# Two interleaved layers of multi-query attention and SwiGLU: chunks turned by VectorE at the layer change, a chunk's operands made earlier, and implied waits declared away

## The chip, the core and the metric

The kernel runs on one core of a Trainium2 chip. The core's engines work in parallel, each through its own queue in order: TensorE (PE: matrix products and transposes; PEld is its weight load), VectorE (DVE), ScalarE (ACT), GpSimd (POOL) and SyncE (SP, which here issues nearly all DMA transfers). Semaphores order the engines against each other; an instruction that waits holds everything behind it in its queue. The metric is the time of one launch on the device in microseconds (us); the median of several runs counts.

## The reference

The input has 2048 rows of 448 numbers. Two kinds of layer alternate, each on a layernorm of the running sum and added to it:

```python
H, Dh, F = 16, 28, 1792
def _A_ref(x, wq, wk, wv, wo):
    q = (x @ wq).reshape(B, S, H, Dh).transpose(0, 2, 1, 3)
    k = x @ wk
    v = x @ wv
    scores = jnp.einsum("bhqd,bkd->bhqk", q, k) * (Dh ** -0.5)
    o = jnp.einsum("bhqk,bkd->bhqd", softmax(scores), v)
    return o.transpose(0, 2, 1, 3).reshape(B, S, H * Dh) @ wo
def _B_ref(x, w_gate, w_up, w_down):
    return (silu(x @ w_gate) * (x @ w_up)) @ w_down

x = x + _A_ref(_layernorm(x), wq, wk, wv, wo)
x = x + _B_ref(_layernorm(x), w_gate, w_up, w_down)
x = x + _A_ref(_layernorm(x), wq, wk, wv, wo)
x = x + _B_ref(_layernorm(x), w_gate, w_up, w_down)
```

The 16 query heads share one key head and one value head. All is float32; the kernel gets that precision by writing operands as a high part and a low part (names ending in `h` and `l`) and adding three products.

## The kernel before

**Tiling.** Rows are on the partitions of `xres` (16 tiles of 128 rows). The rows fall into four chunks of 512. For a product a chunk must be turned: features on partitions, 512 rows along the free axis. This turned form, in halves, is an `xtile`: `xh` and `xl`, and for the feed-forward `xd`, a tile that holds a second copy of the last 64 features on the upper partitions. There are two ways to make one. `flip` has PE transpose 16 blocks of 128x128 (L248) into PSUM; ACT copies the high half out (L254, L258) and DVE subtracts for the low half (L255, L264). `turn_tile` has DVE transpose a tile of rows in blocks of 32x32 (L268), and four DMAs for each tile (L271) write the blocks to DRAM in their turned order; `rows3` reads the chunk back in three DMAs (L130 and two of L132), and `halved` splits it (L278 to L288), on whichever engines it is given.

**The order.** Each engine's order is the order in which the program calls its instructions; it is written out by hand. The stages follow each other: projection, scores, feed-forward, and the same again for the second layer. There is a second, fuller path for inputs whose softmax sums leave a range; it does not run here.

**Scores.** `scores` runs 128 cycles a layer. A cycle (`cycle`) computes two tiles of scores (128 keys by 4 heads of 512 queries each) on PE (L590) into two PSUM groups of three banks, `threes`, and two single banks. ACT takes the exponentials: of the first tile's single bank (L607) and three banks (L608), of the second tile's three banks (L611) and, since DVE has copied it out (L610), its single (L612). `pv(m - 1)` then multiplies the exponentials of the cycle before with the values (P-V, L639) into the single bank that L607 has just read, and DVE adds that to an accumulator (L646, L648). The exponentials go to buffers `pt` and `pt1`, four of each. Every eighth cycle a group of heads ends; `post` normalises it: sums go out to DRAM and come back (L659, L669, L670), POOL multiplies (L677). Some other work is laid between the cycles, by cycle number: the chunks of the feed-forward are normalised and turned by `turn_tile` for chunks 0 to 2, and chunk 1 is read back near the end (`ff.fetch(1)`).

**Feed-forward.** `unit(gi, c, n)` takes one block of 256 of the 1792 hidden features of chunk c: gate and up products in two halves (L318; with L298 for the chunk-0 units at the start, which don't use `xd`), Silu on ACT (L902), products on DVE (L903, L907), a high half on ACT (L904). The down products of a unit are held back in `pend` and run between the halves of the next unit; each block of PE's work ends with tiny ACT copies of its banks into `seen` (L325), for which PE waits before it writes those banks in the other order. After a chunk's second unit of a group the residual is added: two tiles on DVE (L806), two by ACT and POOL (L809, L810). A list `soon` holds functions with a count of units after which they run, at the end of a unit's calls; `mid` holds functions that run in the middle of a given unit. `rest` starts the stage: a shifted copy for chunk 0 by DMA (L127), chunk 1's operands by ACT and DVE, the read of chunk 2 (`fetch(2)`) and its halves on POOL one unit later, chunk 3 by `flip`.

**Layer change.** In the last group (6) of layer 0's feed-forward, `hand_over(c)` normalises a finished chunk (statistics L217, L218; `rstd` on POOL, L222 and L223; scaling L230) for the next layer's projection. Its scaling runs one unit later, by `soon`. For chunks 0 and 1 the `flip` stands in the middle of the unit (6, c + 2, 0), in two halves, and the projections that use it follow (`a.project()`, two for chunk 0, one for chunk 1). Chunk 2 is turned by `flip` inside the projection. A projection (`project`, `q`) is one block of L298 products, copied out by ACT to `stage` (L523, L524), from where SP writes it to DRAM: queries to `qd` (L525), keys to `kt` (L528). `finish` runs what is left of the projection; before that it calls `fetch` twice, which reads four blocks of queries back (`wrq`, L444) and lets POOL cast them (L446) for the products that bound the scores (`maxima`, L424), which come up in `q` at projection 6.

Of the kernel before, what the change touches and what calls it, by code (L numbers as in the profile page):

```python
# [8 lines left out]
F32 = mybir.dt.float32  # L9
# [46 lines left out]
def forward(  # L56
# [209 lines left out]
    def turn_tile(got, tb, raw, t):  # L266

        nc.vector.transpose(tb[:, t, :], got["x"][:, t, 0:D])  # L268
        to = raw.rearrange("(b d) (t g w) -> t g d b w", d=32, g=4, w=32)
        for g in range(4):  # L270
            nc.sync.dma_start(to[t, g], tb[32 * g : 32 * g + 32, t, :].rearrange("d (b w) -> d b w", w=32))  # L271
# [57 lines left out]
    class Attention:  # L329
# [224 lines left out]
        def scores(self, ff):  # L554
            next(switch)
            with tc.tile_pool(name=f"at{self.layer}", bufs=1, reuse_waits="tile") as wp:
                woh = wp.tile([P, NG, D], F32R, name="woh")
                wol = wp.tile([P, NG, D], F32R, name="wol")
# [24 lines left out]
                def tile_scores(n, three, one):  # L583
# [19 lines left out]
                def cycle(m):  # L603
# [3 lines left out]
                    nc.scalar.activation(pt1, a, AF.Exp, scale=SCALE)  # L607
                    nc.scalar.activation(pt, threes[0], AF.Exp, scale=SCALE)  # L608
                    pt, pt1 = tile_scores(2 * m + 1, threes[1], b)
                    nc.vector.tensor_copy(pt1, b)  # L610
                    nc.scalar.activation(pt, threes[1], AF.Exp, scale=SCALE)  # L611
                    nc.scalar.activation(pt1, pt1, AF.Exp, scale=SCALE)  # L612
# [20 lines left out]
                def pv(m, to):  # L633
# [10 lines left out]
                    if u == 0:  # L644
                        accs[i] = halves("o2").bitcast(F32)
                        nc.vector.tensor_copy(accs[i][:, 0, :], to)  # L646
                    else:
                        nc.vector.tensor_tensor(accs[i][:, 0, :], to, accs[i][:, 0, :], ALU.add)  # L648
# [3 lines left out]
                def post(i):  # L652
# [4 lines left out]
                    rs = wp.tile([P, 16], F32, name="rs", bufs=2)  # L657
# [3 lines left out]
                    def rest():  # L661
                        if fine is not None:
                            under = wp.tile([P, 16], F32, name="under", bufs=2)
# [7 lines left out]
                        if g == 0:  # L671
                            on[c] = (
                                wp.tile([P, NG, 512], F32R, name="onh"),
                                wp.tile([P, NG, 512], F32R, name="onl"),
# [11 lines left out]
                def turns(c, got):  # L686
# [3 lines left out]
                    def one(t):  # L690
                        if t == 0:
                            at_["tb"] = wp.tile([P, 4, D], F32, name="tb")
                        turn_tile(got, at_["tb"], ff.raw[c], t)
# [68 lines left out]
    class FeedForward:  # L762
# [61 lines left out]
        def hand_over(self, c):  # L824

            a = self.nxt
            fs, got = norm_steps(c)
# [3 lines left out]
            a.X[c] = xtile(xpool if c == 0 else self.xbp)  # L831

            def ready():
                for f in fs[5:]:
                    f()
                if c > 1:
                    a.norms[c] = got
# [94 lines left out]

        def rest(self, xb):
            self.stage = xb.enter_context(tc.tile_pool(name=f"stage{self.layer}", bufs=2, reuse_waits="tile"))
            self.xbp = xb.enter_context(tc.tile_pool(name=f"xb{self.layer + 1}", bufs=3, reuse_waits="tile"))
# [8 lines left out]
            self.fetch(2)  # L944
            self.soon.append([0, lambda: self.parts(2, nc.gpsimd.tensor_copy, nc.gpsimd.tensor_tensor)])
# [100 lines left out]
```

## Time and profile before

| | |
|---|---|
| runs | 2002.25, 1998.70, 1998.66 us; median 1998.7 |
| profiled execution | 2002.23 us |
| its span, first to last instruction | 2000.5 us |
| granted clock of TensorE | 0.997 |
| projection of layer 0, to | 64 us |
| scores, layer 0 | 64 to 571 us |
| feed-forward, layer 0 | 571 to 1017 us |
| rest of layer 1's projection | 1017 to 1055 us |
| scores, layer 1 | 1055 to 1561 us |
| feed-forward, layer 1 | 1561 to 2000.5 us |

A line of a timeline gives start, duration, engine, line of the kernel, operation, what it writes and reads, and how many of them follow each other; in brackets how long the engine stood idle before it, and for whom. A line of a list of groups gives the count, busy time and mean duration in ns, and the idle time before the group. `SPq` and `ACTq` are instructions of the queues themselves: DMA issues and waits.

### The profile page before, as it was taken

The page shows a single profiled execution, that of the slowest core. Times are in us where ns is not written, and L with a number is a line of the kernel's source. Part 1 is how long each engine was busy: PE and PEld are TensorE (multiplying, and loading weights), DVE is VectorE, ACT ScalarE, POOL GpSimd, SP SyncE. Part 2 cuts the span into 40 slices and gives each one's busy share as a digit, 9 for nine tenths or more (in the row PEclk, how much of TensorE's full clock was granted, in tenths as well). Part 3 has the DMA queues.
Part 4 walks back from the last instruction along what each step waited for, and adds up shares of the span by engine and source line. Part 5 has one row for each costly group of instructions (what it writes and reads, how often), then busy time and mean ns, then how long its engine had stood idle before and what let it go on. Part 6 is the DMA issues. An engine that isn't in the chain of part 4 may idle for free.

```text
span 2000.5 us, 44597 instructions
## 1 busy us (share of the span) xinstructions
PE 1978.4 (99%) x18517; PEld 1337.5 (67%) x18517; DVE 785.4 (39%) x1370; ACT 1277.5 (64%) x2142; POOL 560.4 (28%) x611
## 2 busy tenths in 40 slices
PE   9999999999999999999999999999999999999998
PEld 7544545445468999999884444454454789988887
DVE  6444443443543222322464334535444332222322
ACT  4899797997953333333349998979979433333332
POOL 5222213122214233333351221122221233233320
PEclk9999999999999999999999999999999999999999
DMA  5101020021211011110031010200212100011102
GB/s 164 52 24 37 12 57 17 22 51 32 44 42 35 25 32 31 32 31 22 12 100 35 25 31 12 62 13 26 52 37 58 45 16 22 26 31 32 32 1 76
DMA packets 126343, 75.30 MB, mean 38 GB/s; under 512 B 69656, under 2 KB 109976, under 8 KB 126136
## 3 DMA queue, kind: packets, MB, share of 16 engines
q1 hardware_dynamic: 124584, 71.20, 12.9%
q8 instruction: 146, 2.39, 0.5%
q10 hardware_dynamic: 1552, 1.20, 0.2%
q14 instruction: 61, 0.50, 0.1%
HBM read 54.01 MB, written 17.83 MB: 36 GB/s over the span
## 4 chain that ended last, share of the span: by engine, by line
PE 94%; DVE 2%; POOL 1%; ACT 1%; DMA 1%; issue 0%; ACTq 0%; POOLq 0%; SPq 0%; DVEq 0%
PE bank L318 39%; PE bank L639 24%; PE three L590 17%; PE bank L590 6%; PE bank L298 4%; PE three L575 2%; PE bank L575 2%; PE bank L248 1%; POOL xl L279 0%; DMA qd<-stage 0%; ACT pt L611 0%; DVE xn L230 0%; DMA xn<-xt 0%; DMA xres<-in_A_x_dram 0%; DVE xres L579 0%
## 5 line engine op out<-in xcount | busy, mean ns | idle before, releaser
L639 PE MATMUL bank<-pt,vsb 128*32 128x512 f32 x4096 | 493.2, 598 | 0.5
L590 PE MATMUL bank<-qstack,keys 32*128 32x512 f32 x1536 | 483.8, 424 | 1.7 <-DVE xres L579 1.7
L590 PE MATMUL three<-qstack,keys 32*128 32x512 f32 x4608 | 448.8, 420 | 1.4 <-ACT stage L524 1.0
L318 PE MATMUL bank<-xh,wgh 64*128 64x512 f32 x1728 | 443.7, 391 | 4.0 <-ACT xh L278 1.4
L590 PEld LDWEIGHTS three<-qstack,keys 32*128 32x128 f32 x4608 | 258.1, 182 | 282.2 <-ACT pt L608 185.2
L611 ACT ACTIVATE pt<-three 128x1536 f32<-128x1536 f32 x256 | 383.1, 1496 | 0.0
L608 ACT ACTIVATE pt<-three 128x1536 f32<-128x1536 f32 x256 | 379.4, 1482 | 0.0
L318 PE MATMUL bank<-xh,wgl 64*128 64x512 f32 x1404 | 366.2, 391 | 0.0
L318 PE MATMUL bank<-wdh,h 64*128 64x448 f32 x1792 | 333.1, 365 | 1.2 <-ACT h L904 0.8
L318 PE MATMUL bank<-xl,wgh 64*128 64x512 f32 x1296 | 331.4, 391 | 2.6 <-POOL xl L279 2.1
L903 DVE TENSOR_TENSOR sg<-bank,sg 128x512 f32<-128x512 f32 x112 | 77.5, 692 | 511.8 <-ACT sg L902 502.6
L318 PEld LDWEIGHTS bank<-xh,wgh 64*128 64x128 f32 x1728 | 261.2, 185 | 22.5 <-POOL xh L288 2.2
L639 PEld LDWEIGHTS bank<-pt,vsb 128*32 128x32 f32 x4096 | 107.1, 109 | 249.1 <-issue 152.6
L810 POOL TENSOR_TENSOR xres<-stage,xres 128x448 f32<-128x448 f32 x108 | 127.9, 1204 | 506.0 <-ACT stage L809 506.0
L648 DVE TENSOR_TENSOR o<-bank,o 128x512 f32<-128x512 f32 x224 | 155.0, 692 | 280.5 <-PE bank L639 276.4
L610 DVE COPY pt<-bank 128x512 f32<-128x512 f32 x256 | 176.9, 691 | 205.5 <-PE bank L590 203.1
L318 PEld LDWEIGHTS bank<-wdh,h 64*128 64x128 f32 x1792 | 244.3, 185 | 14.7 <-issue 2.3
L590 PEld LDWEIGHTS bank<-qstack,keys 32*128 32x128 f32 x1536 | 243.9, 183 | 7.8 <-DVE xres L579 3.6
L677 POOL TENSOR_TENSOR o<-o 128x512 f32<-128x512 f32 x32 | 41.2, 1289 | 739.7 <-DMA o<-rd 431.6
L325 ACT COPY seen<-bank 128x1 f32<-128x1 f32 x664 | 81.4, 163 | 255.0 <-PE bank L318 249.8
L318 PEld LDWEIGHTS bank<-xh,wgl 64*128 64x128 f32 x1404 | 214.7, 185 | 13.1
L318 PE MATMUL bank<-wdl,h 64*128 64x448 f32 x896 | 218.2, 368 | 0.0
(130 smaller groups left out, 2323.5 us busy)
## 6 DMA issues: line engine op xcount, KB each, us to landing
o<-rd SPq DMA_DIRECT2D x32, 256.0 KB
qd<-stage SPq DMA_DIRECT2D x32, 224.0 KB
qraw<-qd SPq DMA_DIRECT2D x128, 56.0 KB
wdr<-in_B_w_down_dram SPq DMA_DIRECT2D x28, 224.0 KB
xt<-tb SPq DMA_DIRECT2D x96, 56.0 KB
wr<-in_B_w_gate_dram SPq DMA_DIRECT2D x28, 192.0 KB
wr<-in_B_w_up_dram SPq DMA_DIRECT2D x28, 192.0 KB
xn<-xt SPq DMA_DIRECT2D x6, 768.0 KB
```

What stands on the lines that cost most here:

```text
L298: nc.tensor.matmul(po, a, b, start=(i == 0), stop=(i == len(seq) - 1))
L318: nc.tensor.matmul(po, a, b, start=start, stop=stop, skip_group_check=True)
L325: nc.scalar.copy(seen[:, i : i + 1], po[:, 0:1])
L575: nc.tensor.matmul(po[:, 0:D], a[:, g, ts_], b[:, g, :], start=(g + z == 0), stop=(g == NG - 1 and z == 2))
L590: nc.tensor.matmul(three[:, j, :] if j < 3 else one, k[js, kp, ks], q[js, part, :], start=(z == 0), stop=(z == 2), tile_position=(32 * j, 0),)
L608: nc.scalar.activation(pt, threes[0], AF.Exp, scale=SCALE)
L610: nc.vector.tensor_copy(pt1, b)
L611: nc.scalar.activation(pt, threes[1], AF.Exp, scale=SCALE)
L639: nc.tensor.matmul(to[32 * j : 32 * j + 32, :], vsb[:, n % NT, :], pts[n][j], start=(y == 0), stop=(y == 1), skip_group_check=True,)
L648: nc.vector.tensor_tensor(accs[i][:, 0, :], to, accs[i][:, 0, :], ALU.add)
L810: nc.gpsimd.tensor_tensor(r, s, r, ALU.add)
L903: nc.vector.tensor_tensor(sg, pg[1], sg, ALU.mult)
```

## The change

It has four parts.

1. At the layer change, chunks 0, 1 and 2 are no longer turned by PE. `hand_over` registers two functions for each: `turn` scales the chunk, turns it by `turn_tile` (DVE, then 16 DMAs) into DRAM and reads it back (3 DMAs); `parts` makes the halves by ACT copies and DVE subtractions. They are called one and two units later, chunk 2's `parts` after projection 5. Chunk 0's two projections are called one unit later than before.
2. At the start of both feed-forwards, `begin` makes chunk 1's operands right after the last exponentials, into a pool of their own (`x1`), before the first unit; chunk 2 is read back one unit earlier, in `scores`, and its halves are issued on POOL at the start of `rest`, ahead of the first unit of chunk 1. The shifted copies of chunks 0 and 1 both go by DMA.
3. In the scores the four buffers `pt` and `pt1` are named tiles, taken in turn, and three kinds of dependency are declared absent, with the reason that another wait implies them: between an exponential and the one that wrote the same buffer two cycles before (and DVE's copy L610 likewise), between the accumulator's addition and the one before it, and between it and an exponential of the next cycle.
4. What outlives the scores' buffers (`woh`, `wol`, `rs`, `onh`, `onl`) sits in a pool `ow` on the other side of the memory, so that the pool `at` can be closed ahead of the feed-forward's first unit.

```diff
     def turn_tile(got, tb, raw, t):
-        nc.vector.transpose(tb[:, t, :], got["x"][:, t, 0:D])
+        nc.vector.transpose(tb, got["x"][:, t, 0:D])
...
-        def scores(self, ff):
+        def scores(self, ff, xb):
...
-                    pt = wp.tile([P, 3, 512], F32, name="pt", bufs=4)
-                    pt1 = wp.tile([P, 512], F32, name="pt1", bufs=4)
+                    pt, pt1 = bufs[n % 4]
...
+                exps, sums = {}, {}
+                bufs = [
+                    (wp.tile([P, 3, 512], F32, name=f"pt{y}"), wp.tile([P, 512], F32, name=f"single{y}"))
+                    for y in range(4)
+                ]
...
-                    nc.scalar.activation(pt1, a, AF.Exp, scale=SCALE)
-                    nc.scalar.activation(pt, threes[0], AF.Exp, scale=SCALE)
+                    es = [nc.scalar.activation(pt1, a, AF.Exp, scale=SCALE)]
+                    es.append(nc.scalar.activation(pt, threes[0], AF.Exp, scale=SCALE))
...
+                    exps[m] = [e.ins for e in es]
+                    for new, old in zip(exps[m], exps.get(m - 2, ())):
+                        tc.declare_no_dep(new, old, reason="P-V, which read the buffer, waited for the old one")
+                    if m > 1:
+                        tc.declare_no_dep(copy.ins, exps[m - 2][3], reason="P-V, which read it, waited for that")
...
+                        if m + 1 in exps:
+                            tc.declare_no_dep(f.ins, sums[m - 1], reason="scores, ahead of this P-V, waited for the sum")
+                    sums[m] = f.ins
+                    if m + 1 in exps:
+                        tc.declare_no_dep(f.ins, exps[m + 1][0], reason="P-V waited for the bank's exponential")
...
+                inner.close()
                 next(switch)
                 ff.X[0] = X0
+                ff.begin(xb)
                 ff.unit(0, 0, 0)
                 due.popitem()[1]()
+                ff.fetch(2)
                 ff.unit(0, 0, 1)
...
         def hand_over(self, c):
             a = self.nxt
-            fs, got = norm_steps(c)
+            fs, got = norm_steps(c, twice=c == NC - 1)
...
-            a.X[c] = xtile(xpool if c == 0 else self.xbp)
+            a.X[c] = xtile((xpool, self.x1p, self.xbp, self.xbp)[c])
...
-            self.soon.append([1, ready])
-            if c < 2:
-                self.mid[len(groups) - 1, c + 2, 0] = [lambda ks=ks: flip(got, a.X[c], ks) for ks in ((0, 1), (2, 3))]
-                self.soon.append([2, lambda: [a.project() for _ in range(2 - c)]])
+            raw = dram.tile([D, 512], F32, name=f"xt1_{c}")
+            def turn():
+                for f in fs[5:]:
+                    f()
...
+                for t in range(4):
+                    turn_tile(got, self.tb[t // 2][:, t % 2, 0:D], raw, t)
+                got["raw"] = pers.tile([P, 4, 512], F32, name="xn")
+                rows3(got["raw"], raw)
+            def parts():
+                halved(a.X[c], got["raw"], range(4), nc.scalar.copy, nc.vector.tensor_tensor)
+            self.soon.append([1, turn])
+            if c == 2:
+                a.plan[5, 1] = [parts]
+                return
+            self.soon.append([2, parts])
+            self.soon.append([3 - c, lambda: [a.project() for _ in range(2 - c)]])
...
+        def begin(self, xb):
+            self.x1p = xb.enter_context(tc.tile_pool(name=f"x1{self.layer}", bufs=1, reuse_waits="tile"))
+            self.X[1] = xtile(self.x1p)
+            halved(self.X[1], self.got.pop(1), range(4), nc.scalar.copy, nc.vector.tensor_tensor)
+
         def rest(self, xb):
...
-            dma(self.xd[0][64:128, :], self.X[0][0][0:64, 3, :])
-            self.X[0] = (*self.X[0][:2], self.xd[0])
-            self.parts(1, nc.scalar.copy, nc.vector.tensor_tensor)
+            for c in range(2):
+                dma(self.xd[c][64:128, :], self.X[c][0][0:64, 3, :])
+                self.X[c] = (*self.X[c][:2], self.xd[c])
...
-            self.fetch(2)
-            self.soon.append([0, lambda: self.parts(2, nc.gpsimd.tensor_copy, nc.gpsimd.tensor_tensor)])
+            self.parts(2, nc.gpsimd.tensor_copy, nc.gpsimd.tensor_tensor)
```

More of the change, by code (lines that the diff above doesn't have):

```diff
@@ L552, in finish @@
             wide.append(LOW)
-        def scores(self, ff):
+        def scores(self, ff, xb):
             next(switch)
-            with tc.tile_pool(name=f"at{self.layer}", bufs=1, reuse_waits="tile") as wp:
-                woh = wp.tile([P, NG, D], F32R, name="woh")
-                wol = wp.tile([P, NG, D], F32R, name="wol")
+            inner = ExitStack()
+            with tc.tile_pool(name=f"ow{self.layer}", bufs=1, side="right", reuse_waits="tile") as ow:
+                wp = inner.enter_context(tc.tile_pool(name=f"at{self.layer}", bufs=1, reuse_waits="tile"))
+                woh = ow.tile([P, NG, D], F32R, name="woh")
+                wol = ow.tile([P, NG, D], F32R, name="wol")
                 on, accs, pts = {}, {}, {}
```

34 lines of the change are left out of this document (19 added, 15 removed).

## The prediction

> **What bounds the kernel now.** I read the page's chain of waits first.
>
> ```profile
> span 2000.5 us, 44597 instructions
> PE 94%; DVE 2%; POOL 1%; ACT 1%; DMA 1%; issue 0%; ACTq 0%; POOLq 0%; SPq 0%; DVEq 0%
> ```
>
> PE is in 94% of the chain that ended last, so work that leaves PE counts in full, and a wait counts where PE stands in it. The scores are a quarter of the program each time, and there I looked closer: at the busy time of the engines in one stretch of them (us; PE, its weight loads, DVE, ACT, POOL), at ACT's timeline, and at the list of the single tile's exponential L607.
>
> ```profile
> 80.00:197.00 117.00, 117.00 (x1273) 50.07 (x1269) 46.83 (x84) 117.00 (x127) 23.09 (x21) 1.00 0.09 24
> ...
> L607 ACT ACTIVATE pt<-bank x33: 604/654/700, 79.7 to 197.7; 128x512 f32<-128x512 f32 x33
> ...
> L607 ACTq EVENT_SEMAPHORE  x254: 17/17/1029, 64.2 to 1556.6; - x127
> ...
> 68.69 0.63 ACT L607 ACTIVATE pt<-bank 128x512 f32<-128x512 f32 x1
> 76.01 0.68 ACT L607 ACTIVATE pt<-bank 128x512 f32<-128x512 f32 x1
> ```
>
> PE and ACT are both busy for all 117 us, so the first row doesn't tell which of them sets the period of a cycle (four exponentials, two tiles). The starts do. Between 79.7 and 197.7 us lie 32 periods, 3.688 us each; the two cycles from 68.69 to 76.01 took 3.66 each. PE's work is the same in both. What the early cycles lack are ACT's waits on itself: the exponentials of cycles 0 and 1 write fresh buffers, and the waiting instructions of L607 number 254 to its 256 exponentials. So ACT, with its waits, sets the period.
>
> **The change part by part.**
>
> *Waits in the scores.* They go from some 126 cycles of each layer: 252 x (3.688 - 3.660) = -6.9 us. Bounds: 0, if PE's P-V after L607's end turns out to be what closes the period, and -8.2 (.0325 a cycle, if the rounding of the starts is all on one side).
>
> *A new wait in layer 0.* The first three-bank exponential now writes a buffer that lies where the projection's staging tile lay, and waits until the last key copy out of it (L528) has landed.
>
> ```profile
> 65.51 1.47 ACT L608 ACTIVATE pt<-three 128x1536 f32<-128x1536 f32 x1
> ...
> 65.72 0.39 SPq L528 DMA_DIRECT2D kt<-stage  x1
> 68.16 0.55 SPq L383 DMA_DIRECT2D wrk<-kt  x1
> ```
>
> That copy is issued at 65.72, and SP's next instruction, which waits for it, goes at 68.16: landed at about 68.0, so the exponential starts 2.5 us late, once. Behind it in ACT's queue stands the whole cycle, and P-V waits for that: +2.5. (0, if PE's work ahead covered it; 3 at most.) In layer 1 the corresponding copies are down in time.
>
> *Start of each feed-forward.* Today PE runs into waits here, on ACT's copy of chunk 1 and on POOL's halves of chunk 2.
>
> ```profile
> 593.71 0.37 PE L575 MATMUL bank<-woh,onl 128*128 128x448 f32 x1
> 594.78 0.50 PE L318 MATMUL bank<-xh,wgh 64*128 64x512 f32 x2 [0.71 <-ACT xh L278]
> 612.90 0.50 PE L318 MATMUL bank<-xl,wgh 64*128 64x512 f32 x2 [1.07 <-POOL xl L279]
> 622.21 0.39 PE L318 MATMUL bank<-xh,wgh 64*128 64x512 f32 x1
> ...
> 1584.42 0.37 PE L575 MATMUL bank<-woh,onl 128*128 128x448 f32 x1
> 1614.12 0.39 PE L318 MATMUL bank<-xh,wgh 64*128 64x512 f32 x1
> ...
> 960.42 0.57 PE L318 MATMUL bank<-xh,wgh 64*128 64x512 f32 x2
> 964.18 0.57 PE L318 MATMUL bank<-xh,wgh 64*128 64x512 f32 x2
> 967.72 0.57 PE L318 MATMUL bank<-xh,wgh 64*128 64x512 f32 x2
> ```
>
> The last three rows, far from any stall, give the normal unit: 7.30 us, 3.76 for its first gate-up half with a down-projection and 3.54 for its second. From the end of the last output projection (593.71 + .37 = 594.08) three units should bring PE to 615.98; it gets there at 622.21, so 6.2 us are lost. Layer 1: 1584.79 + 21.9 = 1606.69 against 1614.12, 7.4 lost. After the change chunk 1's operands are made right behind the last exponentials, while PE multiplies the first unit's weights, so the wait on ACT's L278 goes. Chunk 2's halves are made by POOL from here on:
>
> ```profile
> 600.81 1.01 POOL L223 TENSOR_TENSOR rstd<-rstd,halfn 128x4 f32<-128x4 f32 x1
> 606.52 0.61 POOL L278 CAST xh<-xn 128x512 fp32r<-128x512 f32 x1
> 609.14 1.29 POOL L279 TENSOR_TENSOR xl<-xn,xh 128x512 fp32r<-128x512 f32 x1
> 611.06 1.78 POOL L279 TENSOR_TENSOR xl<-xn,xh 128x512 fp32r<-128x512 f32 x1
> 614.26 1.26 POOL L288 TENSOR_TENSOR xh<-xn,xd 64x512 fp32r<-64x512 f32 x1
> ...
> 611.03 0.69 DVE L907 TENSOR_TENSOR h<-sg,h 128x512 fp32r<-128x512 f32 x1 [0.69 <-ACT h L904]
> ```
>
> They take 606.52 to 615.52, 9.0 us. POOL now issues them right behind L223 and ahead of the residual adds. DVE's statistics lose the four operations ahead of them, so L223 ends some 2.9 us sooner than 601.82: about 598.9, and the halves are ready at 607.9. PE begins with chunk 2 at 594.08 + 2 x 7.30 = 608.7 and, in the order of the rows, wants the last of them some .4 later, near 609.1. What is late next is chunk 1's shifted copy (L127), now behind chunk 0's: issued some .8 after the last output projection's start, landed 2.3 later (as the key copy above) near 596.8, .4 after PE's first use, in each layer. Sum: -(6.2 + 7.4) + .9 = -12.7. Bounds -13.6 and -10.
>
> The row at 611.06 is .49 longer than its like at 609.14, and DVE's product L907 starts beside it at 611.03. [...]
>
> *The hand-over to layer 1.* First what goes: 48 PE transposes and their evictions, in three lumps.
>
> ```profile
> 978.20 0.49 PE L298 MATMUL bank<-xh,wh 128*128 128x512 f32 x1
> 983.43 0.49 PE L318 MATMUL bank<-xh,wgh 64*128 64x512 f32 x2
> 1007.77 0.39 PE L318 MATMUL bank<-xh,wgh 64*128 64x512 f32 x2
> 1025.07 1.10 PE L424 MATMUL bank<-q,kdiag 112*128 112x512 f32 x4
> 1026.00 1.91 PE L248 MATMUL bank<-ident,xn 128*128 128x128 f32 x16
> 1027.67 0.48 PE L298 MATMUL bank<-xh,wh 128*128 128x512 f32 x1
> ```
>
> The unit from 967.72 to 978.20 holds chunk 0's lump: 10.48 - 7.30 = 3.2. Chunk 1's, of the same 16 and two such splits of a unit, I take at the same or a little less, 3.0 (an estimate); chunk 2's is 1027.67 - 1026.00 = 1.7. Together -7.9.
>
> In their place stands, for each chunk, a chain across four queues: DVE's scaling and four transposes, 16 writes and 3 reads on SP, four copies on ACT, four subtractions on DVE. Its pieces are all in the trace, because chunks of the feed-forward go this way already:
>
> ```profile
> 969.48 1.77 DVE L230 TENSOR_SCALAR xn<-xres,mv,rstd 128x448 f32<-128x448 f32 x4
> L268 DVE STREAM_TRANSPOSE tb<-xn 128x448 f32<-128x448 f32 x24 | 15.2, 635 | 0.0
> 288.64 2.25 SPq L271 DMA_DIRECT2D xt<-tb  x4
> 292.31 0.39 SPq L130 DMA_DIRECT2D xn<-xt  x1
> 1588.16 4.75 DMA xn<-xt
> ...
> 984.56 0.42 SPq L528 DMA_DIRECT2D kt<-stage  x1
> 1015.38 2.07 SPq L444 DMA_DIRECT2D wrq<-qd  x4
> 1022.29 2.02 POOL L446 CAST q<-wrq 112x1024 fp32r<-112x1024 f32 x2
> 1015.99 0.47 PE L318 MATMUL bank<-wdh,h 64*128 64x448 f32 x1 [0.18 <-ACT seen L325]
> ```
>
> From scaling to the first turned tile 1.77 + .64 = 2.4; 16 writes at 2.25 / 4 = .56 or, with nothing between them, less, 8.3; from the last write's end to the reads 292.31 - 290.89 = 1.4; the third read goes 1.0 later and lands in 4.75; the last copy .6, the `seen` copies behind it .5. About 19.7 us from the start of scaling.
>
> The place decides what that costs. The copies stand in ACT's queue ahead of the `seen` copies (L325), and PE's second gate-up half waits for those (the last row shows such a wait). Chunk 0: scaling at 969.48, copies through at 989.2. Without its lump PE would reach that half at 967.72 + 7.30 + 3.76 = 978.8. Stall 10.4 (9.8 to 10.9): the two projections (978.20 to 983.43) that could have covered 5.2 of it are moved behind it. Chunk 1: counted from that half's start, its writes can go on SP only behind the copies of those projections: 3.5 to the pair, 6.4 to its last copy (984.56 - 978.20) and .4 for that, 10.3. Then 8 for the writes, 1.5, 1.0, 4.8, and copies to 27.4 or 28.4; PE needs it at 3.5 + 5.2 + 7.3 + 2.6 + 3.8 = 22.5. Stall 5.3 (4.3 to 5.8). Chunk 2: the 16 writes and 3 reads go ahead of the four wrq reads on SP, and behind these stand POOL's L446 and PE's L424, which today runs 17.3 after the last unit's second half starts (1007.77). The writes can start 7.5 after it; with 8 for them, 1.4 until they are down, 1.6 for the reads, .4 for a query copy, 2.1 for the wrq reads, some 3.0 for landing (between the 2.3 of the key copy above and the 4.75) and 1.0 for the last L446, L424 goes at 25.0. Against 17.3, stall 7.7 (6.7 to 8.3). In all 23.4 - 7.9 = +15.5, between 13 and 17.5. POOL's 12 copies L232 go too; nothing waited for them.
>
> **Sum.** +15.5 - 12.7 + 2.5 - 6.9 = -1.6 us. The profiled execution took 2002.23 for its span of 2000.5; its span would be 1998.9. The other two runs took 1998.7, so the profiled one lies 3.5 high; on the median I predict 1998.7 - 1.6 = 1997.1 us.
>
> **The rivals.**
>
> *PE closes the period of the scores (slower).* P-V (L639) is queued ahead of the scores that feed the next L607, and waits for L607: a loop through both engines, and PE is as full as ACT in the stretch above. If that loop, not ACT's row of four, is 3.69 long, it keeps its length and the waits buy nothing: -1.6 + 6.9 = +5.3, 2004.0. It decides if the period stays above 3.68. Against it stand the cycles of 3.66.
>
> *The hand-over costs less (faster).* If PE finds L424 late by nothing, since SP has other slack or the next projections can run ahead of it, chunk 2's 7.7 go: -9.3, 1989.4. For it: PE is in one queue with much work left in that stage; against: L424 stands in that queue where it is, and the wrq reads can't pass the writes on SP.
>
> *The change doesn't do what it says at the feed-forward's start.* If POOL's halves still end where they do, for want of L223 or of the read that is now issued earlier, only the first waits there go, 1.4 a layer: -1.6 + 12.7 - 2.8 = +8.3, 2007.0. The reads are issued some 15 us earlier, so I see little for it.
>
> **How the numbers follow.** The forecast has .48, the cheaper hand-over .26, the scores' loop .18, the late halves .08. No change is told from one within 0.2%, 4 us, of the median: 1994.7 to 2002.7. The forecast's own range is 1992 to 2001, with a quarter of it below 1994.7; faster gets .26 + .12 = .38, slower .08 + .12 of the loop's case + .02 of the forecast's = .22, same the other .40. The range from 1988 to 2006 leaves out half of the late halves and the outermost of the cheap hand-over.
>
> **What would show it.** In the list of exponentials a period of 3.66 right through the layer, not 3.69. At layer 0's first cycle a gap of 2.5 between the first two exponentials. No PE wait on POOL's halves in the first three units of either feed-forward. In the last group of layer 0's feed-forward two stalls of PE on ACT's `seen` copies, 10 and 5 us, and one of about 8 ahead of L424. The forecast is wrong if one of the three large terms is: if the stalls lie elsewhere or are hidden, or the period stays.

## The result, and the profile after

The changed kernel takes 2018.2 us (median of 4 runs, 2016.96 to 2018.95) against 1999.9 for the kernel before (4 runs, 1998.66 to 2002.25): 1.0086 times as long, 95% interval 1.0074 to 1.0098. The prediction was 1997.1 and its range ended at 2006. The profiled execution took 2018.01 us; its span is 15.8 us longer than before, where -1.6 was forecast.

The page after: span, the clock granted to PE in 40 slices of the span (9 is 90% or more), and the chain by engine.

```profile
span 2016.3 us, 43622 instructions
...
PEclk9999999999999999999889999999999999999999
...
PE 95%; DMA 2%; DVE 1%; ACT 1%; issue 0%; SPq 0%; POOL 0%; ACTq 0%; DVEq 0%; POOLq 0%
```

The chain looks as before. What is new is a dent in the granted clock, in the two slices from 958 to 1059 us: the layer change.

Where the time went is read by putting the starts of the same instructions side by side, from the two timelines. Whatever lies between two rows of this table gained or lost the difference of its last column.

| instruction | before, us | after, us | after minus before |
|---|---|---|---|
| first exponential of layer 0 | 65.02 | 65.46 | +0.4 |
| the same of cycle 2 | 72.35 | 76.69 | +4.3 |
| the same of the last cycle, 127 | 565.95 | 568.99 | +3.0 |
| Silu of unit (0,2,0), layer 0 | 621.18 | 618.83 | -2.3 |
| Silu of unit (6,1,1) | 966.86 | 964.52 | -2.3 |
| Silu of unit (6,2,0) | 977.08 | 971.81 | -5.3 |
| Silu of unit (6,2,1) | 989.82 | 991.98 | +2.2 |
| Silu of unit (6,3,0) | 1000.04 | 1005.14 | +5.1 |
| Silu of unit (6,3,1) | 1010.28 | 1023.35 | +13.1 |
| first exponential of layer 1 | 1055.62 | 1079.50 | +23.9 |
| the same of the last cycle | 1556.64 | 1579.17 | +22.5 |
| Silu of unit (0,2,0), layer 1 | 1613.09 | 1629.03 | +15.9 |
| end | 2000.50 | 2016.29 | +15.8 |

So the starts of the two feed-forwards gain 5.4 and 6.6, 12.0 together (12.7 forecast), the scores 1.3 a layer (6.9 forecast for both), the first cycles lose 3.9 (2.5), and the layer change loses 26.2 (15.5). Outside these places the two kernels run in step to .2 us.

The layer change first. These are the waits of PE there (us in total, times, longest), then the row of PE after the first of them, and below it four stretches: their length, busy time of PE, PEld, DVE, ACT and POOL, then the granted clock.

```profile
PE bank L318 <- ACT seen L325: 16.4, 3, 10.5
PE bank L424 <- POOL q L446: 8.3, 1, 8.3
PE bank L298 <- DVE xres L826: 1.4, 1, 1.4
```

```profile
987.30 0.80 PE L318 MATMUL bank<-xh,wgh 64*128 64x512 f32 x2 [10.54 <-ACT seen L325]
987.90 0.63 PE L318 MATMUL bank<-xl,wgh 64*128 64x512 f32 x2
988.32 0.63 PE L318 MATMUL bank<-xh,wgl 64*128 64x512 f32 x2
```

```profile
987.20:990.00 2.80, 2.69 (x12) 2.17 (x14) 1.00 (x2) 0.38 (x5) 0.00 (x0) 0.50 0.00 0
993.00:997.00 4.00, 4.00 (x21) 3.10 (x20) 3.31 (x8) 1.20 (x2) 0.00 (x0) 1.00 0.02 4
1018.60:1022.00 3.40, 3.33 (x16) 2.64 (x18) 1.23 (x2) 0.34 (x5) 0.93 (x4) 0.50 0.26 73
1048.50:1052.00 3.50, 3.41 (x8) 2.74 (x9) 3.29 (x7) 0.11 (x1) 0.03 (x1) 0.50 0.56 173
```

The same rows of the same unit in the kernel before:

```profile
987.31 0.39 PE L318 MATMUL bank<-xh,wgh 64*128 64x512 f32 x2
987.54 0.39 PE L318 MATMUL bank<-xl,wgh 64*128 64x512 f32 x2
987.77 0.40 PE L318 MATMUL bank<-xh,wgl 64*128 64x512 f32 x2
```

The three stalls are there, on the waits that the prediction named, with nearly its sizes: 10.5 on the `seen` copies (10.4 forecast), 5.7 on them again (5.3), 8.3 ahead of L424 (7.7). But behind each of them the granted clock of PE is half of full. After the first it is at .50 until 992.8, for 5.5 us, with steps of .42 to .43 us between rows where the same rows before were .23 apart; then it is at 1.0. After the second it lasts 4.8 us, after the third 5.6. So a stall of 10.5 us costs more than 10.5 us: from the Silu of unit (6,2,0) to that of (6,2,1) pass 20.2 us, the unit's 7.3, the 10.5 and 2.3 more, and the next unit begins in the last .8 us of the half clock.

The first cycle of layer 0, in ACT's timeline, and the clock of the stretch that follows:

```profile
65.46 0.61 ACT L614 ACTIVATE single<-bank 128x512 f32<-128x512 f32 x1
68.66 1.45 ACT L615 ACTIVATE pt<-three 128x1536 f32<-128x1536 f32 x1 [2.59 <-DMA kt<-stage]
```

```profile
71.80:74.50 2.70, 2.70 (x20) 0.95 (x20) 0.69 (x1) 2.70 (x4) 0.62 (x1) 0.50 0.22 61
77.00:80.00 3.00, 3.00 (x37) 0.99 (x29) 1.25 (x2) 3.00 (x4) 0.00 (x0) 1.00 0.00 0
```

The wait for the key copy came as forecast, 2.6 us. Here too the clock fell to half behind it, and the next cycle but one began another 1.2 late.

The scores, as the list of the first exponential shows them over the same stretch, before (L607) and after (L614):

```profile
L607 ACT ACTIVATE pt<-bank x22: 604/645/693, 120.2 to 197.7; 128x512 f32<-128x512 f32 x22
```

```profile
L614 ACT ACTIVATE single<-bank x22: 742/752/760, 120.8 to 198.2; 128x512 f32<-128x512 f32 x22
```

21 periods take 77.5 us before and 77.4 after: 3.690 and 3.686. The waits are gone (of the 254 waiting instructions of this line 6 are left in the whole program), and the period stayed. What did change is the duration of the exponential, 645 to 752 ns: it starts earlier and ends when it did. The timeline of ACT after one of its pauses shows how:

```profile
227.22 0.64 ACT L614 ACTIVATE single<-bank 128x512 f32<-128x512 f32 x1
230.87 0.67 ACT L614 ACTIVATE single<-bank 128x512 f32<-128x512 f32 x1
234.53 0.69 ACT L614 ACTIVATE single<-bank 128x512 f32<-128x512 f32 x1
```

By starts the period is 3.655. By ends (227.86, 231.54, 235.22) it is 3.68. From cycle to cycle the starts run further ahead of the ends: the exponential takes .64, .67 and .69 us here, and .75 at 319 us, where the starts too are 3.68 apart.

At the start of the feed-forward, finally, this is all that PE waits for from 569 to 625 us, and the row of the wait:

```profile
PE bank L318 <- DMA xd<-xh: 0.2, 1, 0.2
```

It is the shifted copy of chunk 1, .2 us late where .4 was forecast; no wait on POOL's halves is left. Layer 1 has the same single wait, of .2.

### The profile page after: what moved, and what is told of

Same layout as the page of the kernel before. It is cut to its first block, busy times and chain, and to the rows that moved or that the text cites. A ratio compares the mean times of both kernels' runs of the same rounds, so it can differ in the third digit from the quotient of the medians.

```text
span 2016.3 us, 43622 instructions
## 1 busy us (share of the span) xinstructions
PE 1972.0 (98%) x18469; PEld 1301.1 (65%) x18469; DVE 790.2 (39%) x1382; ACT 1275.6 (63%) x2140; POOL 556.3 (28%) x599
## 4 chain that ended last, share of the span: by engine, by line
PE 95%; DMA 2%; DVE 1%; ACT 1%; issue 0%; SPq 0%; POOL 0%; ACTq 0%; DVEq 0%; POOLq 0%
PE bank L318 39%; PE bank L651 24%; PE three L592 20%; PE bank L298 4%; PE bank L592 3%; PE three L577 2%; PE bank L577 2%; DMA xn<-xt 1%; DMA qd<-stage 1%; PE bank L248 0%; PE bank L424 0%; DMA xt<-tbp 0%; SPq L271 0%; DMA xd<-xh 0%; DVE xres L581 0%
## 5 line engine op out<-in xcount | busy, mean ns | idle before, releaser
L651 PE MATMUL bank<-single,vsb 128*32 128x512 f32 x1024 | 488.1, 599 | 0.0
L592 PE MATMUL bank<-qstack,keys 32*128 32x512 f32 x1536 | 471.1, 425 | 1.7 <-DVE xres L581 1.7
L318 PE MATMUL bank<-xh,wgh 64*128 64x512 f32 x1728 | 451.5, 392 | 16.2 <-ACT seen L325 16.2
L592 PE MATMUL three<-qstack,keys 32*128 32x512 f32 x4608 | 462.3, 425 | 3.7 <-ACT pt L615 2.4
L592 PEld LDWEIGHTS three<-qstack,keys 32*128 32x128 f32 x4608 | 252.0, 183 | 297.4 <-ACT pt L615 187.7
L618 ACT ACTIVATE pt<-three 128x1536 f32<-128x1536 f32 x256 | 409.2, 1598 | 0.0
L615 ACT ACTIVATE pt<-three 128x1536 f32<-128x1536 f32 x256 | 405.6, 1584 | 2.6 <-DMA kt<-stage 2.6
L318 PE MATMUL bank<-xh,wgl 64*128 64x512 f32 x1404 | 371.9, 392 | 0.0
L318 PE MATMUL bank<-xl,wgh 64*128 64x512 f32 x1296 | 338.3, 392 | 0.0
L942 DVE TENSOR_TENSOR sg<-bank,sg 128x512 f32<-128x512 f32 x112 | 77.5, 692 | 510.7 <-ACT sg L941 506.5
L651 PEld LDWEIGHTS bank<-pt,vsb 128*32 128x32 f32 x3072 | 101.8, 109 | 261.1 <-issue 153.2
L617 DVE COPY single<-bank 128x512 f32<-128x512 f32 x256 | 177.0, 691 | 211.6 <-PE bank L592 206.1
L318 PEld LDWEIGHTS bank<-xh,wgl 64*128 64x128 f32 x1404 | 218.6, 185 | 15.9
```

The costliest lines, as they stand in the source:

```text
L318: nc.tensor.matmul(po, a, b, start=start, stop=stop, skip_group_check=True)
L592: nc.tensor.matmul(three[:, j, :] if j < 3 else one, k[js, kp, ks], q[js, part, :], start=(z == 0), stop=(z == 2), tile_position=(32 * j, 0),)
L615: es.append(nc.scalar.activation(pt, threes[0], AF.Exp, scale=SCALE))
L617: copy = nc.vector.tensor_copy(pt1, b)
L618: es.append(nc.scalar.activation(pt, threes[1], AF.Exp, scale=SCALE))
L651: nc.tensor.matmul(to[32 * j : 32 * j + 32, :], vsb[:, n % NT, :], pts[n][j], start=(y == 0), stop=(y == 1), skip_group_check=True,)
```

## The experiments

Two theories stood at the start. One: the layer change costs its three stalls and, behind each, a slow restart of PE; the scores are bound by ACT's own work. The other, for the excess of the layer change: something in the rest of the change (tiles in other places, the order on SP) makes it dear; and for the scores: the waits do cost, or PE is the bound.

**The old hand-over in the changed kernel.** `hand_over` as before (chunks 0 and 1 by `flip` in the middle of a unit, chunk 2 in the projection), all else of the change kept.

```diff
-            self.soon.append([1, turn])
...
-            self.soon.append([2, parts])
-            self.soon.append([3 - c, lambda: [a.project() for _ in range(2 - c)]])
+            self.soon.append([1, ready])
+            if c < 2:
+                self.mid[len(groups) - 1, c + 2, 0] = [lambda ks=ks: flip(got, a.X[c], ks) for ks in ((0, 1), (2, 3))]
+                self.soon.append([2, lambda: [a.project() for _ in range(2 - c)]])
```

> The changed kernel with the old hand-over: chunks 0 to 2 turned by PE again, everything else of the change kept. By the comparison of the two traces the hand-over (from the Silu of unit (6,1,1), 964.5 us, to the first exponential of layer 1) costs 26.2 us more than before, so the span should be 2016.3 - 26.2 = 1990.1 us, 10 below the kernel before: -12.2 from the two starts of the feed-forward, -2.6 from the scores, +4.3 from the first cycle. Rival: part of the 26 us comes from the moved memory or the earlier start of chunk 1, and stays; then the span stands above 1993.

Measured: span 1989.9 us; 1994.2 in the median of 5 runs against 2002.2 for the kernel before on that chip, 0.9961 (0.9947 to 0.9975). From the Silu of unit (6,1,1) to the first exponential of layer 1 pass 88.4 us, against 88.8 in the kernel before and 115.0 in the changed one: the layer change alone makes the changed kernel slower, and without it the change is a gain. That the forecast of the span holds to .2 us is in part luck, since the profiled run is the fastest of the five; the spans of the others are 1991.5 to 1993.0.

**The new hand-over alone.** The kernel before with only this part of the change, `turn` and `parts` as the diff of the change has them.

```diff
-            self.soon.append([1, ready])
+            self.soon.append([1, turn])
...
+            self.soon.append([2, parts])
+            self.soon.append([3 - c, lambda: [a.project() for _ in range(2 - c)]])
```

> The kernel before with only the new hand-over. If the parts of the change add up, the span is 2000.5 + 26.2 = 2026.7 us (2025 to 2028). If the new hand-over suffers from the other parts (tiles in other places, another order on SP), it costs less here, and the span stays under 2024.

Measured: span 2025.1, one run of 2026.9 us. It adds 24.6 us here (25.6 up to the first exponential of layer 1) and 26.2 there: the parts add up, and the other tiles' places are not what makes it dear.

**The waits back in the scores.** As the first experiment, without the three declarations.

```diff
-                    for new, old in zip(exps[m], exps.get(m - 2, ())):
-                        tc.declare_no_dep(new, old, reason="P-V, which read the buffer, waited for the old one")
-                    if m > 1:
-                        tc.declare_no_dep(copy.ins, exps[m - 2][3], reason="P-V, which read it, waited for that")
...
-                            tc.declare_no_dep(f.ins, sums[m - 1], reason="scores, ahead of this P-V, waited for the sum")
...
-                        tc.declare_no_dep(f.ins, exps[m + 1][0], reason="P-V waited for the bank's exponential")
```

> As the first of these four, but with the three declarations of absent dependencies left out, so that ACT waits on itself again in the scores. Theory now: ACT's own work sets the period, 3.685 us from end to end, and its waits are taken while the exponential before is still running; then the span is that of the first run to within 1 us, or up to 2.6 above it if the declarations are what took the longer third cycles (3.725) away. The prediction's theory, that waits cost .0275 a cycle, asks for 6.9 more.

Measured: 1993.9 us in the median of 5 runs, 0.9959 (0.9945 to 0.9973), the same as with the declarations. In the profile the same stretch of the scores has this row:

```profile
L614 ACT ACTIVATE single<-bank x22: 597/652/677, 121.4 to 199.1; 128x512 f32<-128x512 f32 x22
```

77.7 us for 21 periods, 3.700, against 3.686 without the waits: between cycle 2 and cycle 127 the layers lose 1.1 and 1.0 us. (The profiled span, 1992.8, is 2.9 longer; 2.0 of it arose in cycle 1, behind the wait for the key copy, where the clock fell to .50 here.) So the declarations are worth some 2 us by the profiles, which the medians of the runs can't tell from nothing, and not 6.9.

**Without the fourth exponential.** As the first experiment, but with the exponential L619 left out, and the one declaration that names it.

```diff
-                    es.append(nc.scalar.activation(pt1, pt1, AF.Exp, scale=SCALE))
```

> The kernel with the old hand-over and the rest of the change (span 1989.9 us), with the last of the four exponentials of each cycle left out: the second tile's single is only copied by VectorE, and P-V multiplies the raw scores of that head. Theory: ACT's own time from end to end (1.34 + 1.34 + .52 + .49 = 3.69) sets the period; without the .52 it falls to 3.17, or to what PE needs by itself if that is more; a period under 3.60 decides for ACT. Rival, as the prediction's: PE, or the loop of PE through the first exponential, sets 3.69; then the period stays above 3.65 and the span within 3 us of 1989.9.

The sums leave their range without it, so the second path ran as well and the time of the launch (8907 us) says nothing; the first path's scores can be read.

```profile
L614 ACT ACTIVATE single<-bank x31: 597/599/602, 80.1 to 189.5; 128x512 f32<-128x512 f32 x31
...
  PE bank L592: 11.2, 31
```

30 periods take 109.4 us, 3.65 each, and now ACT stands idle ahead of each first exponential (31 times, 11.2 us) until PE's scores are there, while PE is busy for 109.3 of the 109.4 us. So neither limit of the expectation decides: with ACT's work cut by .52 us, the period falls by .04, to what PE allows. ACT sets it with all four exponentials, but PE is only 1% behind; no change to waits could have bought more than .04 a cycle.

**PE kept busy in the stalls.** The changed kernel with idle transposes on PE: into a free bank before the second half of units (6,2,1) and (6,3,1), and into L424's bank.

```diff
+                if self.nxt and gi == len(groups) - 1 and c > 1 and n == 1:
+                    mid = [lambda: None, lambda c=c: keep_busy(banks[next(b for b in LOW if b not in live)], 80 if c == 2 else 36)]
...
+            if self.layer and c == 0:
+                keep_busy(pm, 60)
```

> The changed kernel with idle transposes on PE in the three stalls of the hand-over: 80 in the first (10.5 us), 36 in the second (5.7), 60 in front of the first L424 (8.3), some .1 us each, so that they end before what PE waits for is there. Theory: after each stall PE runs some 5 us at half its granted clock, which costs 2.3 us each time; kept busy it starts at full clock, the granted clock in the 3 us after each stall is 1.0 and not .5, and the span falls by 5 to 7 us, to 2009 to 2011. Rival: the slow start has to do with the operands or the queues after the wait; then the matmuls after the stall are still .43 us apart and the span stays at 2016.

Measured: span 2015.6, one run of 2017.4 us. The rows of PE behind the first two stalls, and the clock of the 3 us behind each of the three:

```profile
987.36 0.49 PE L318 MATMUL bank<-xh,wgh 64*128 64x512 f32 x2 [1.57 <-ACT seen L325]
...
1017.80 0.79 PE L318 MATMUL bank<-xh,wgh 64*128 64x512 f32 x2 [3.11 <-ACT seen L325]
```

```profile
987.40:990.40 3.00, 3.00 (x27) 2.51 (x29) 0.85 (x2) 0.65 (x5) 0.00 (x0) 1.00 0.00 0
1017.80:1020.80 3.00, 3.00 (x14) 2.40 (x16) 1.16 (x2) 0.27 (x4) 0.94 (x4) 0.50 0.27 78
1049.00:1052.00 3.00, 2.90 (x13) 2.40 (x14) 1.99 (x5) 0.11 (x1) 0.05 (x1) 1.00 0.52 152
```

The first stall ends at the same time as in the changed kernel, 987.3, and the unit behind it is 2.1 us shorter, the next one .4: the restart is the clock, not the operands. Behind the second, where PE still stood idle for 3.1 us, the clock was half again; behind the third, also after 3.1 us, it was full. But the layer change is only 1.6 us shorter and the span .7, not 5: chunk 1's writes took longer and the wrq reads landed later, and ate the rest. A second run, with 80, 60 and 84 transposes; its edit against the run before:

```diff
-                    mid = [lambda: None, lambda c=c: keep_busy(banks[next(b for b in LOW if b not in live)], 80 if c == 2 else 36)]
+                    mid = [lambda: None, lambda c=c: keep_busy(banks[next(b for b in LOW if b not in live)], 80 if c == 2 else 60)]
...
-                keep_busy(pm, 60)
+                keep_busy(pm, 84)
```

> The changed kernel with idle transposes in all three stalls again, now 80, 60 and 84, so that PE stands still for less than 2 us before each goes on. In the run with 80, 36 and 60 the clock was full after the first and third stall and half after the second, where PE had stood still for 3.1 us; but the span fell by only .7, since chunk 1's writes on SP took 9.9 us and not 8.6, and the wrq reads landed later. If those delays were chance, the span is now 2016.3 - 7 = 2009 to 2011, with a granted clock of 1.0 after all three stalls; if they come with the transposes, the clock is full and the span stays at 2014 to 2016.

Measured: span 2013.3; 2015.2 us in the median of 4 runs, 1.0076 (1.0059 to 1.0093) of the kernel before. The clock is 1.0 behind all three. The layer change is 3.3 us shorter than in the changed kernel, not 7: 2.6 came behind the first stall, .6 behind the second and .1 behind the third. At the second, SP's issue of chunk 1's writes took this:

```profile
996.66 9.96 SPq L271 DMA_DIRECT2D xt<-tbp  x16
```

against 8.63 us in the changed kernel. It did so in both runs with transposes. All of the excess is in one of the sixteen issues, as their shortest, median and longest durations show (in ns; the changed kernel first):

```profile
L271 SPq DMA_DIRECT2D xt<-tbp x16: 303/488/538, 1000.3 to 1008.5; - x16
L271 SPq DMA_DIRECT2D xt<-tbp x16: 303/484/1855, 996.7 to 1006.2; - x16
```

In both runs a packet of 16 KB on the queue q8, which the profile's page lists under "instruction", starts .09 us into the long issue and takes 1.34 and 1.35 us; in the changed kernel none falls into these writes. Packets of this queue fill 8% of the time, and yet in the traces of the kernel before and the changed kernel 28 of the 29 issues longer than 1.2 us have one in them. So the delay goes with these packets; why one falls there in both runs is open. Ahead of the third stall the run lost something else, for behind PE's wait for the residual the clock fell:

```profile
PE bank L298 <- DVE xres L833: 1.5, 1, 1.5
...
1028.00:1031.00 3.00, 3.00 (x8) 2.35 (x8) 2.36 (x8) 1.81 (x2) 2.28 (x2) 0.50 0.68 105
```

In the changed kernel it was full there. What is shown is the slow clock behind each stall, and 2.6 us for it at the first.

**Chunk 1's halves later.** The changed kernel with chunk 1's `parts` one unit later, when its data have landed.

```diff
-            self.soon.append([2, parts])
+            self.soon.append([2 + c, parts])
```

> The changed kernel with chunk 1's halves made one unit later, after the Silu of unit (6,3,1), when its data have landed; the projection needs them only from projection 4 on. Theory: the second stall (5.65 us) and the slow clock after it (2.3) go, and VectorE reaches chunk 2's scaling up to 2 us later in its order: span 2016.3 - 6 to - 8, 2008 to 2011. Rival: the stall only moves to the chain behind it (chunk 2's writes, the wrq reads, L424), and the span stays above 2014.

Measured: span 2010.4, one run of 2012.1 us: 5.9 off the span, within the forecast of 2008 to 2011. Its waits of PE at the layer change:

```profile
PE bank L318 <- ACT seen L325: 10.7, 2, 10.5
PE bank L424 <- POOL q L446: 6.6, 1, 6.6
PE bank L298 <- DVE xres L826: 4.2, 1, 4.2
```

The second stall is gone with its restart (8.0 at the Silu of unit (6,3,1): 5.7 and 2.3), and 3.4 come back behind it; another 1.1 went at the first stall, where the half clock lasted 2.9 us and not 5.5. The place of the copies in ACT's queue was the cause.

**The wrq reads first.** The changed kernel with chunk 2's 16 writes and 3 reads called after the two `fetch` calls, its `parts` after projection 7.

```diff
+                self.writes()
...
             if c == 2:
-                a.plan[5, 1] = [parts]
+                a.plan[7, 1] = [parts]
```

> The changed kernel with chunk 2's 16 writes and 3 reads behind the four wrq reads on SP instead of ahead of them, and its halves made after projection 7. Theory: the wait ahead of L424 (8.3) goes to under 1 us, which shows that it was the place on SP. But writes, reads and halves take some 18 us from there, and PE has four projections of 2.6 us until projection 8 needs chunk 2: a stall of 5 to 9 us appears there. Span 2012 to 2016. If the chain were quicker than that, 2006.

Measured: span 2020.1, one run of 2021.8 us, slower than the changed kernel by 3.8. The wait ahead of L424 is no longer listed; this one is:

```profile
PE bank L299 <- ACT xh L279: 11.9, 1, 11.9
```

The mechanism held (SP's order caused the wait at L424), and a stall takes its place as forecast, but it is 11.9 and not 5 to 9, so the forecast of 2012 to 2016 was missed. The chain is simply longer than the work that PE has left.

**Another buffer in the first cycle.** As the first experiment, with the buffers taken as 1, 2, 3, 0.

```diff
-                    pt, pt1 = bufs[n % 4]
+                    pt, pt1 = bufs[(n + 1) % 4]
```

> The kernel with the old hand-over and the rest of the change, with the four exponential buffers taken in the order 1, 2, 3, 0, so that the one over the staging tile comes up only at the second half of cycle 1. Theory: the first two exponentials of layer 0 are .49 us apart instead of 3.2, and the span falls by 2.7 from 1989.9 to 1987.2 (2 more where a slow clock followed the gap). Rival: the wait is for something else in the pool, and stays.

Measured: span 1989.1, one run of 1990.9 us. In layer 0 the first cycle is 2.7 us shorter, as the theory says; but by cycle 2 of layer 1 all of what layer 0 had gained, 3.4, is lost again: PE waits .8 and 1.4 us around the first exponential there, and then the clock is at .50 from 1050.8 to 1057.6. What the first wait there is for is not shown. A miss by one layer. So the next version takes that order in layer 0 alone, `bufs[(n + (self.layer == 0)) % 4]`:

> The old hand-over with the rest of the change, and the exponential buffers in the order 1, 2, 3, 0 in layer 0 alone; layer 1 keeps 0, 1, 2, 3, since the other order met a wait there. Theory: only the 2.7 us of layer 0's first cycle go; span 1989.9 - 2.7 = 1987.2 (1986 to 1988). Rival: the wait comes back at another place, 1989 or more.

Measured: span 1986.4; 1988.0 us in the median of 4 runs, 0.9935 (0.9917 to 0.9953) of the kernel before, the shortest time of all versions here. The spans of the four runs lie within .5 us. All that PE waits for from 945 to 1060 us:

```profile
PE bank L592 <- DVE single L617: 0.4, 1, 0.4
PE three L592 <- ACT stage L524: 0.3, 1, 0.3
PE bank L318 <- ACT seen L325: 0.2, 1, 0.2
```

**Chunk 0 alone by VectorE, with time.** That version with chunk 0 turned by VectorE, its halves and its projections one unit later than in the change.

```diff
+                self.soon.append([1, turn])
+                self.soon.append([3, lambda: halved(a.X[0], got["raw"], range(4), nc.scalar.copy, nc.vector.tensor_tensor)])
+                self.soon.append([4, lambda: [a.project() for _ in range(2)]])
```

> As the one before, with chunk 0 alone turned by VectorE at the layer change, its halves made one unit later than in the change (after the Silu of unit (6,2,1)) and its projections after unit (6,3,0). Theory: the chain of 19.7 us has its time there: the data land near 985 with PE at that point needing ACT's seen copies near 986, so PE waits at most 1 us, and the 3.2 us of chunk 0's PE transposes go: 1984 to 1985.2. Rival: PE waits for the copies again, 2 us or more and a slow restart with it, and the span is above 1987.

Measured: span 1991.7; 1993.8 us in the median of 6 runs, 0.9962 (0.9949 to 0.9975). The wait on ACT's copies is indeed .5 at most, but the forecast of 1984 to 1985.2 was missed; PE waits elsewhere:

```profile
PE bank L248 <- DVE xn L230: 6.1, 1, 6.1
```

There is one tile `xn`. Chunk 1's scaling writes it and so must stand behind chunk 0's subtractions, which read it, and these wait for the chain. The expectation had looked at ACT's queue only.

**Chunks 0 and 1 by VectorE, with time.** The same for both.

```diff
-            if c == 0:
+            if c < 2:
...
-                self.soon.append([4, lambda: [a.project() for _ in range(2)]])
+                self.soon.append([4 - 2 * c, lambda: [a.project() for _ in range(2 - c)]])
```

> As the one before, with chunk 1 turned by VectorE too, its halves after the Silu of unit (6,3,1). Theory: another 3.0 us of PE transposes go and up to 2 come back, since ACT's copies stand ahead of the last unit's seen copies and VectorE reaches chunk 2's scaling later: 1981 to 1984. Rival: as chunk 1's 16 writes and 3 reads go ahead of the query copies and the wrq reads on SP, L424 waits, and the span is above 1986.

Measured: span 1994.5; 1996.0 us in the median of 10 runs, 0.9972 (0.9962 to 0.9982). That misses the forecast, 1981 to 1984, and the rival's wait ahead of L424 isn't there either: PE waits 7.4 us on the `seen` copies, 3.7 at the longest. Turning by PE stays the better way at this place.

## Why the prediction was wrong

*The hand-over*, the largest term, had the right waits and the wrong price. The three stalls were forecast at 10.4, 5.3 and 7.7, on the right waits, and measured 10.5, 5.7 and 8.3; the lump that goes with chunk 0 at 3.2, measured 2.9. The step that failed is "In all 23.4 - 7.9 = +15.5", where 23.4 are the three stalls: it prices a stall at the time that PE stands still. Behind each stall PE ran at half clock. Of the 26.2 measured, 24.5 are stalls, 1.4 a wait for the residual (L826) that was not forecast, and -7.9 (as forecast) what went; the 8.2 that remain are the three restarts and some tenths. The half clock lasted 5.5, 4.8 and 5.6 us behind the three; with rows .43 apart instead of .23 that is an estimated 7.4 us. The first restart is shown by the runs that kept PE busy (2.6), the second by the run with chunk 1's halves later (2.3); for the third the clock was made full, but what it is worth by itself isn't shown, since other things moved in those runs. The rows for it were in the trace before, where PE waits for POOL's halves in layer 1:

```profile
1606.29 0.79 PE L318 MATMUL bank<-xh,wgh 64*128 64x512 f32 x1 [0.54 <-POOL xh L288]
...
1606.20:1609.00 2.80, 2.71 (x14) 2.58 (x16) 1.78 (x4) 0.48 (x3) 1.53 (x5) 0.50 0.00 0
```

The matmul takes .79 us instead of .50, at half clock. The prediction went past it, because at that place it measured from end to end.

*The waits in the scores* were the second step that failed: "252 x (3.688 - 3.660) = -6.9". The early cycles have a shorter period by their starts, because ACT's starts run ahead of its ends at first. The two rows that carried the step say so themselves, once their durations are added: 68.69 + .63 and 76.01 + .68 are 7.37 apart, 3.685 a cycle, against 3.688 in the 32 after them. So the early cycles lacked nothing. The runs showed some 2 us for the declarations. The rival, a loop through PE, came nearer in size (0, with 2.6 measured) for the wrong reason: with one exponential less the period falls, so PE alone was not what closed it.

*The wait in layer 0* was right in place and size (2.6 for 2.5), with the same omission: the clock fell behind it, and 1.2 were added.

*The start of the feed-forward* was right: 12.0 for 12.7, no wait on POOL left, .2 for the shifted copy. It had the restarts in its price without knowing of them: in the kernel before the clock was at .50 for 3.4 us there in layer 0 and for 6.8 us in layer 1, and a sum from end to end holds that.

Together: 10.7 for the hand-over, 4.3 for the scores, 1.4 for the first cycle and .7 for the feed-forward, with .4 ahead of the first exponential, are the 17.4 between -1.6 and +15.8, to a tenth. The rival with a cheaper hand-over had no ground: SP's order did reach PE. None of the rivals had the hand-over dearer, and that was the gap in the range: every bound of that term was made from the same rows, with the same omission.

## What to carry to other kernels

A stall of PE, where PE sets the end, can cost more than its length (here 10.5 us and 2.3 more behind it): look at the granted clock in the microseconds behind a stall that the trace already has, and put that restart into the price of each new one. Read the period of back-to-back work from ends, not from starts (3.68 and 3.655 here), before a difference between two starts is multiplied by hundreds of cycles. And a step moved off the busy engine needs room for its whole chain at the place where it is called, through every queue and every shared tile: here a chain of 20 us (967.14 to 987.30 for chunk 0) took the place of some 3 us of transposes, and each attempt to move the wait only found the next one.

## What the runs showed of the hardware that was not expected

Behind an idle time of PE of 10.5, 5.7 and 8.3 us the granted clock was .50 in the changed kernel. For shorter waits their length doesn't decide it. After 3.1 us it was .50 once and 1.0 once in the same execution; in the first cycle of layer 0, where ACT waits 2.59 us for the key copy in the changed kernel and 2.56 us in the first experiment, it was .50 behind the wait in the one and 1.0 in the other; it was .50 behind a wait of 1.5 us in the last run with transposes; and in layer 1 of the kernel before it was .50 from 1604.97 us on, behind waits of 1.07 and .60 us.

The two waits of 3.1 us in one execution, the run with 80, 36 and 60 transposes, in these rows: PE did nothing in either stretch, and the clock fell within the first (.86 in its mean) and stayed full in the second.

```profile
1014.70:1017.80 3.10, 0.00 (x0) 0.00 (x0) 2.15 (x4) 2.83 (x9) 0.00 (x0) 0.86 0.01 1
1046.00:1049.00 3.00, 0.00 (x0) 0.00 (x0) 2.12 (x3) 1.28 (x3) 1.51 (x2) 1.00 0.55 145
```

What decides whether it falls is not shown by these runs.

Four exponentials of 512, 512, 1536 and 1536 columns follow each other every 3.68 to 3.70 us by their ends, with ACT's waits or without, while their starts may be 3.655 apart for some five cycles after a pause.
